# Value, query and key weights loaded ahead of input blocks, five filler products fewer, and new instruction orders

## The chip, the cores and the metric

The kernel runs on one core of a Trainium2 chip. The metric is the device time of one execution in microseconds (us). The core has TensorE (PE in the profile, with PEld for its weight loads), VectorE (DVE), ScalarE (ACT), GpSimd (POOL) and SyncE (SP), which here issues the DMA transfers. Each engine takes its instructions in the order in which they stand, and waits at an instruction until the semaphores it names have come.

## What is computed

Two different layers, each run twice, on 2048 tokens of 448 numbers in bf16. Layer A is attention with 16 heads of 28, in which a token sees eight tokens, two apart, up to itself; layer B is a gated product of width 1792:

```python
def _A_ref(x, wqkv, wo):
    ...
    qkv = (lambda x, *d: x.transpose(*d))((x @ wqkv).reshape(B, S, 3, H, Dh), 2, 0, 3, 1, 4)
    ...
    attn = _softmax(logits, axis=-1)
    o = jnp.einsum("bhsw,bhswd->bhsd", attn, vg)
    return (lambda x, *d: x.transpose(*d))(o, 0, 2, 1, 3).reshape(B, S, D) @ wo

def _B_ref(x, w_gate, w_up, w_down):
    ...
    h = g * u
    return jnp.einsum("bsf,fd->bsd", h, w_down)

x = A_x
x = x + _A_ref(_layernorm(x, axis=-1), A_wqkv, A_wo)
x = x + _B_ref(_layernorm(x, axis=-1), B_w_gate, B_w_up, B_w_down)
x = x + _A_ref(_layernorm(x, axis=-1), A_wqkv, A_wo)
x = x + _B_ref(_layernorm(x, axis=-1), B_w_gate, B_w_up, B_w_down)
return x
```

## The kernel before

The tokens are cut into 16 blocks of 128, held in `x_sb`, and the blocks into chunks (lines 57 and 58): the first layer A has chunks of 256, 512, 512, 512 and 256 tokens, so that chunk 0 is blocks 0 and 1 and chunk 1 is blocks 2 to 5. The line `SEQ` names in which order the chunks of the four layers are gone through. For a chunk of layer A the program does the following.

- Layer norm (`ln_chunk`, from line 582): DVE takes the statistics of each block (L592, L594), ACT makes the scale of two blocks from them by a logarithm and an exponential (L595, L597), DVE writes the normalised block twice into `xn_sb` (L616). In the first layer, PE transposes the block (L631 for the first chunk, with the whole array, L635 for the others, with half of it), and ACT or DVE copies it to `xnTa` (L642, L645).
- Queries and keys (`qk_chunk`, from line 698): four units of 14 products, each in two parts of 6 and 8 products (L355), 256 or 512 columns wide like the chunk, out of `xnTa` and `WQK`. Two products run side by side on the two halves of the array. ACT or DVE takes the result from PSUM to `qk` (L730).
- Values (`v_group`, from line 752): 14 products out of `xnTa` and `WV` in the same two parts, for one or two query blocks of 120 tokens, taken out by L795, L804, L809 and L822.
- Attention (`attn_front`, `attn_back`, `norm`): bursts of 32 or 64 small products (L855, L889) with exponentials on ACT (L864), masks on DVE (L871), and a normalisation by L918 to L939. Then the output projection out of `wo_g` or `wo_h` (`y_blocks`).

A chunk of layer B (`b_chunk`, from line 990) has gate and up products out of `WGU`, their product on ACT and DVE (L1013, L1019), and the down projection out of `WD`.

The weights for queries and keys come to a staging place in `hT` in four loads, one for each group of input rows ("piece" below: c is 1, 3, 0, 2 for the operations 3, 4, 5, 6; L468, shown as L450 by the profile since all plain loads are issued by that helper). Eight copies spread them into `WQK` with gaps for 32-wide heads (L517, two for each piece), on ACT or on DVE, as the order says. Every query and key product of the chunk waits for all eight. Four more copies (L525) rewrite parts of `WQK` once chunks 0 and 1 have read them.

Before there is anything to multiply, PE runs products on zeros, `WARM` of them as a start and `FILL` more as fillers (L509).

No scheduler decides at run time. `ORDER` (line 105) lists for each engine the numbers of the operations in the order in which they are emitted, and `BANKS` (line 162) names the PSUM banks of each of PE's operations; both are tables written out in the file. `schedule` reads them; a bank's next user waits for the operation that gives it back. In PE's table, `a*2.4.5/b:2+c:1` splits the burst `a` after so many groups of eight products and puts there the first steps of `b` and `c` as eight narrow strips each (L358). In SP's table the operations 0, 1, 2 and 7 load blocks 0, 1, 2 to 3 and 4 to 7 of the input, 13 and 12 load blocks 12 to 15 and 8 to 11, 8 and 9 load the value weights, and 3 to 6 the query and key weights. Operations are numbered as they are added, so with five fillers fewer every number behind them falls by five.

Of the kernel before, what the change touches and what calls it, by code (L numbers as in the profile page):

```python
# [59 lines left out]
FILL = 9  # L60
# [37 lines left out]
def grp_nc(g):  # L98
# [21 lines left out]
    ),  # L120
    "act": (
# [262 lines left out]
def build(nc, A_x, A_wqkv, A_wo, B_w_gate, B_w_up, B_w_down, out):  # L384
# [122 lines left out]
    fill = None  # L507
    for n in range(WARM + FILL):
        sc.add("pe", one(lambda E, n=n: E.matmul(ps[:, n % NBK if n < NBK else wb[0], :], warm[:, 0:128], warm, start=True, stop=True), ("warm", n)), 427.0 if n < WARM else 216.0, deps=["c_warm"], mode="F",  # L509
               acquire=wb if n == 0 else None, release=[(wb, 0)] if n == WARM + FILL - 1 else [], prio=-100 if n < WARM else 100, after=fill)  # L510
        fill = sc.ops[-1]
# [650 lines left out]
```

## Time and profile before

| | us |
|---|---|
| median of 3 runs | 379.52 (379.10 to 379.61) |
| the profiled execution | 380.59 |
| its span, from the first to the last instruction | 378.9 |
| PE busy in it | 373.2 |
| DVE busy | 271.6 |
| ACT busy | 199.3 |

The profile is of a single execution. Its times are microseconds from the start of its span; a row of a timeline gives start, duration, engine, line, operation, tiles and how many instructions of that kind follow each other, and in brackets how long the engine was idle before them and what released it. A row of the chain of waits gives start, duration and what stood there. Durations of neighbours overlap: an engine begins the next instruction before the last one's end, so prices are taken from start to start where rows allow it.

### The profile page before, as it was taken

What the parts mean: (1) busy time and instruction counts of PE and PEld (TensorE: products, weight loads), DVE (VectorE), ACT (ScalarE), POOL (GpSimd) and SP (SyncE); (2) the same over time, 40 slices, a digit from 0 to 9 for tenths busy, and PEclk for the clock granted to TensorE, in tenths of its full rate; (3) what the DMA queues carried; (4) which work ended last, traced back from release to release, by engine and by line L of the source; (5) the groups of instructions that cost most, each with busy time, mean ns of one, the idle gap of its engine ahead of it and who ended that gap; (6) DMA issues with size and microseconds to landing.
All of it is one profiled execution on the core that took longest, in us unless ns stands there. A gap on an engine that the chain in (4) does not pass through costs nothing.

```text
span 378.9 us, 14223 instructions
## 1 busy us (share of the span) xinstructions
PE 373.2 (99%) x6372; PEld 208.2 (55%) x6372; DVE 271.6 (72%) x564; ACT 199.3 (53%) x333; POOL 5.2 (1%) x25
## 2 busy tenths in 40 slices
PE   8999999999999999999999999999999999999997
PEld 3554678544544445455766756554455454444864
DVE  6999989988786385867477978528897587275233
ACT  4898786657444565444466413556766544123310
POOL 5000000000000000000000000000000000000000
DMA  7767464610414023022102125220026104103002
GB/s 248 179 139 150 55 185 132 111 23 21 82 22 69 5 55 72 20 48 55 24 10 52 39 43 100 49 51 21 20 32 95 39 3 90 44 2 74 2 13 98
DMA packets 59892, 24.38 MB, mean 64 GB/s; under 512 B 49016, under 2 KB 59704, under 8 KB 59832
## 3 DMA queue, kind: packets, MB, share of 16 engines
q1 hardware_dynamic: 59688, 23.42, 29.0%
q8 instruction: 50, 0.82, 0.9%
q14 instruction: 10, 0.08, 0.1%
q10 hardware_dynamic: 144, 0.06, 0.1%
HBM read 9.04 MB, written 3.50 MB: 33 GB/s over the span
## 4 chain that ended last, share of the span: by engine, by line
PE 92%; ACT 4%; DMA 2%; SPq 1%; DVE 1%; issue 0%; DVEq 0%
PE ps L355 84%; PE ps L358 4%; PE ps L855 2%; ACT qk L730 2%; PE ps L889 2%; DMA hT<-in_A_wqkv_dram 2%; PE ps L1031 1%; SPq L450 1%; ACT E_sb L864 1%; ACT v_sb L822 0%; ACT R_sb L919 0%; ACT R_sb L920 0%; ACT O_sb L900 0%; DVE WQK L517 0%; DVE Qz L841 0%
## 5 line engine op out<-in xcount | busy, mean ns | idle before, releaser
L355 PE MATMUL ps<-xnTb,WGU 64*128 64x512 bf16 (+1 forms) x1902 | 171.6, 332 | 0.8 <-ACT R_sb L920 0.8
L355 PEld LDWEIGHTS ps<-xnTb,WGU 64*128 64x128 bf16 x1902 | 92.2, 94 | 70.3 <-issue 1.5
L1013 ACT ACTIVATE g_sb<-ps 128x512 bf16<-128x512 f32 x112 | 65.8, 596 | 90.7 <-PE ps L355 86.4
L1019 DVE TENSOR_TENSOR hT<-g_sb,ps 128x512 bf16<-128x512 bf16 x112 | 75.1, 681 | 40.1 <-ACT g_sb L1013 38.8
L355 PE MATMUL ps<-WD,hT 64*128 64x448 bf16 x786 | 80.5, 349 | 0.0
L980 DVE TENSOR_TENSOR x_sb<-x_sb,ps 128x448 bf16<-128x448 bf16 x62 | 36.3, 615 | 30.1 <-PE ps L355 29.8
L355 PEld LDWEIGHTS ps<-WD,hT 64*128 64x128 bf16 x786 | 37.7, 94 | 33.7 <-DVE hT L1019 0.2
L355 PE MATMUL ps<-xnTa,WQK 64*128 64x512 bf16 (+1 forms) x496 | 52.6, 353 | 0.5 <-DVE WQK L517 0.2
L864 ACT ACTIVATE E_sb<-ps,shift_sb 128x1024 bf16<-128x1024 f32 (+1 forms) x36 | 37.2, 1068 | 11.7 <-PE ps L855 11.7
L592 DVE BATCH_NORM_STATS2 st<-x_sb 128x6 f32<-128x448 bf16 x64 | 38.2, 618 | 1.4 <-DMA x_sb<-in_A_x_dram 1.2
L355 PEld LDWEIGHTS ps<-xnTa,WQK 64*128 64x128 bf16 x496 | 22.7, 94 | 22.6 <-DVE O_sb L904 1.0
L730 ACT ACTIVATE qk<-ps 128x1024 bf16<-128x1024 f32 (+1 forms) x28 | 25.4, 931 | 17.5 <-PE ps L355 17.1
L616 DVE TENSOR_SCALAR xn_sb<-x_sb,mv,rstd 128x512 bf16<-128x512 bf16 (+1 forms) x64 | 27.6, 455 | 4.9 <-ACT rstd L597 4.9
L871 DVE TENSOR_TENSOR E_sb<-E_sb,MK 128x1024 bf16<-128x1024 bf16 (+1 forms) x36 | 23.4, 658 | 9.0 <-ACT E_sb L864 8.9
L355 PE MATMUL ps<-wo_g,oT 64*128 64x448 bf16 x151 | 26.0, 350 | 0.0
L355 PE MATMUL ps<-WV,xnTa 64*128 64x336 bf16 (+3 forms) x244 | 23.6, 304 | 0.4 <-DMA WV<-in_A_wqkv_dram 0.4
L919 ACT ACTIVATE R_sb<-R_sb 128x960 f32<-128x960 f32 (+1 forms) x18 | 17.3, 961 | 11.4 <-DVE R_sb L918 11.4
L918 DVE STREAM_SHUFFLE R_sb<-O_sb 128x960 f32<-128x960 f32 (+1 forms) x18 | 21.2, 1180 | 0.0
L900 ACT ACTIVATE O_sb<-ps 128x448 f32<-128x448 f32 (+2 forms) x27 | 13.9, 548 | 11.5 <-PE ps L889 11.3
L939 DVE TENSOR_TENSOR oT<-O_sb,R_sb 128x960 bf16<-128x960 f32 (+1 forms) x16 | 17.5, 1095 | 3.2 <-ACT R_sb L920 3.2
L595 ACT ACTIVATE lnv<-mv,eps_sb 128x2 f32<-128x2 f32 (+1 forms) x33 | 9.2, 292 | 20.0 <-DVE mv L594 17.7
L920 ACT ACTIVATE R_sb<-R_sb 128x960 f32<-128x960 f32 (+1 forms) x18 | 17.3, 959 | 0.3
(67 smaller groups left out, 243.2 us busy)
## 6 DMA issues: line engine op xcount, KB each, us to landing
out_dram<-x_sb SPq DMA_DIRECT2D x15, 112.0 KB, 1.8
x_sb<-in_A_x_dram SPq DMA_DIRECT2D x3, 448.0 KB, 7.4
hT<-in_A_wqkv_dram SPq DMA_DIRECT2D x4, 224.0 KB, 5.5
WGU<-in_B_w_gate_dram SPq DMA_DIRECT2D x4, 224.0 KB, 4.1
WGU<-in_B_w_up_dram SPq DMA_DIRECT2D x4, 224.0 KB, 3.8
WD<-in_B_w_down_dram SPq DMA_DIRECT2D x2, 448.0 KB, 4.2
mv_rows<-oT SPq DMA_DIRECT2D x12, 64.0 KB, 1.7
oT<-mv_rows SPq DMA_DIRECT2D x48, 8.0 KB
```

Source lines behind the costliest of these rows:

```text
L355: return lambda E: E.matmul(out(), lhs(), rhs(), start=start, stop=stop)
L592: sc.add("dve", one(lambda E, B=B: E.bn_stats(st6[:, B, :], x_sb[:, B, :]), ("bn", li, B)), 525.0, deps=[("x", li - 1, B)] + ([("xn", li - ...
L616: sc.add("dve", one(lambda E, B=B, dst=dst, src=src: E.tensor_scalar(dst, src, mv[:, B, 0:1], rstd[:, B:B + 1], ALU.subtract, ALU.mult), ( ...
L730: return E.activation(dst, src, ACT.Copy) if hasattr(E, "activation") else E.tensor_copy(dst, src)
L864: return E.activation(E_sb[:, slot, 2 * hp:2 * hp + 2, 0:w], ps[:, b0:b0 + 2, 0:w], ACT.Exp, bias=shift_sb[:, 0:1], scale=SCALE)
L871: return E.tensor_tensor(e, e, MK[:, kind, 0:nc].unsqueeze(1).unsqueeze(1).to_broadcast([128, 2, w // nc, nc]), ALU.min)
L918: sc.add("dve", one(lambda E: E.stream_shuffle(R, Of, [DH] * 32), ("Rs", li, qb)), dve_est(w) + 20.0, deps=[("Oa", li, g)] + prev, prio=prio)
L919: sc.add("act", one(lambda E: E.activation(R, R, ACT.Ln), ("Rl", li, qb)), act_est(w, False), deps=[("Rs", li, qb)], prio=prio)
L939: return E.tensor_tensor(dst, O.rearrange("p d h n -> p h d n"), Rv.rearrange("p d h n -> p h d n"), ALU.mult)
L980: sc.add("dve", one(lambda E: E.tensor_tensor(x_sb[:, B, :], x_sb[:, B, :], ps[:, bk[w], 0:D], ALU.add), ("x", li, B)), dve_est(D), deps=[ ...
L1013: sc.add("act", one(lambda E, gs=gs, bk=bk: E.activation(g_sb[:, gs, :], ps[:, bk[0], :], ACT.Copy), ("G", li, j, f0)), act_est(512), deps ...
L1019: return E.tensor_tensor(hT[:, f0:f0 + nf, hs, 0:nt], v(g_sb[:, gs, :]), v(ps[:, bk[1], :]), ALU.mult)
```

## The change

Outside of `FILL`, `ORDER` and `BANKS` no line differs. PE has 13 products on zeros instead of 18. The orders of PE, ACT, DVE and SP and the banks are written anew; the order of POOL is as it was.

```diff
 WARM = 9
-FILL = 9
+FILL = 4
 YP = 8
...
     "sp": (
-        "0 1 2 7 8 9 5 4 6 3 13 72 12 74 73 10 11 75 76 77 78 196 79 80 198 81 86 84 87 85 71 83 334 336 293 92 82 538 467 333 335 469 89 468 345 91 88 344 466 "
...
+        "0 1 8 9 2 5 4 6 3 7 13 67 12 69 68 10 11 70 71 72 73 74 75 191 76 193 81 79 82 80 66 78 77 331 288 84 328 329 330 340 87 86 533 535 461 463 83 464 339 "
```

Line numbers behind the tables are one higher in the changed kernel (L355 becomes L356). First SyncE's first instructions, the loads: `x_sb` are input blocks, `WV` value weights, `hT` the staged query and key weights. Before:

```order
L450 DMA x_sb<-in_A_x_dram 128x448 x2
L450 DMA x_sb<-in_A_x_dram 128x2x448
L450 DMA x_sb<-in_A_x_dram 128x4x448
L450 DMA WV<-in_A_wqkv_dram 128x2x448 x2
L450 DMA hT<-in_A_wqkv_dram 128x896 x4
L450 DMA x_sb<-in_A_x_dram 128x4x448
L450 DMA WGU<-in_B_w_gate_dram 64x2x896
```

Now:

```order
L451 DMA x_sb<-in_A_x_dram 128x448 x2
L451 DMA WV<-in_A_wqkv_dram 128x2x448 x2
L451 DMA x_sb<-in_A_x_dram 128x2x448
L451 DMA hT<-in_A_wqkv_dram 128x896 x4
L451 DMA x_sb<-in_A_x_dram 128x4x448 x2
L451 DMA WGU<-in_B_w_gate_dram 64x2x896
```

The value weights went ahead of blocks 2 and 3 and of blocks 4 to 7, and the four weight pieces ahead of blocks 4 to 7, which are now the tenth load instead of the fourth (of the two 128x4x448 in the row, the second is blocks 12 to 15, where it was). The next loads stand where they stood.

Then PE from its start to the first wide query and key products. L509 are the products on zeros, L631 and L635 transposes of input blocks, rows with `WV` value products, rows with `WQK` query and key products. Before:

```order
L509 MATMUL ps<-hT 128x512 x14
L631 MATMUL ps<-hT,xn_sb 128x128 x8
L509 MATMUL ps<-hT 128x512 x4
L355 MATMUL ps<-WV,xnTa 128x224 x6
L635 MATMUL ps<-hT,xn_sb 128x64 x8
L355 MATMUL ps<-WV,xnTa 128x224 x8
L635 MATMUL ps<-hT,xn_sb 128x64 x16
L355 MATMUL ps<-WV,xnTa 128x448 x6
L635 MATMUL ps<-hT,xn_sb 128x64 x8
L355 MATMUL ps<-WV,xnTa 128x448 x8
L355 MATMUL ps<-xnTa,WQK 128x256 x6
L355 MATMUL ps<-xnTa,WQK 128x512 x6
```

Now:

```order
L510 MATMUL ps<-hT 128x512 x11
L632 MATMUL ps<-hT,xn_sb 128x128 x4
L510 MATMUL ps<-hT 128x512
L632 MATMUL ps<-hT,xn_sb 128x128 x4
L510 MATMUL ps<-hT 128x512
L356 MATMUL ps<-WV,xnTa 128x224 x14
L636 MATMUL ps<-hT,xn_sb 128x64 x16
L356 MATMUL ps<-WV,xnTa 128x448 x14
L356 MATMUL ps<-xnTa,WQK 128x256 x20
L636 MATMUL ps<-hT,xn_sb 128x64 x16
L356 MATMUL ps<-xnTa,WQK 128x256 x14
L356 MATMUL ps<-xnTa,WQK 128x512 x42
```

Before, the transposes of blocks 2 to 5 (32 products of L635) stood between the value products, ahead of all query and key products. Now those of blocks 2 and 3 (16) stand there, and those of blocks 4 and 5 (the second row of 16) behind the first 20 query and key products.

Last ACT, behind the scales of the first two blocks: L642 and L645 copy transposed blocks, L517 copies query and key weights, L795, L804, L809 and L822 take values out of PSUM. Before:

```order
L595 ACTIVATE lnv<-mv,eps_sb 128x2
L597 ACTIVATE rstd<-lnv 128x2
L645 ACTIVATE xnTa<-ps 128x4x128
L795 ACTIVATE v_sb<-ps 128x4x28
L645 ACTIVATE xnTa<-ps 128x4x128 x3
L795 ACTIVATE v_sb<-ps 128x8x28
L595 ACTIVATE lnv<-mv,eps_sb 128x2
```

Now:

```order
L643 ACTIVATE xnTa<-ps 128x4x128 x2
L596 ACTIVATE lnv<-mv,eps_sb 128x2
L598 ACTIVATE rstd<-lnv 128x2
L518 ACTIVATE WQK<-hT 128x16x28 x3
L796 ACTIVATE v_sb<-ps 128x4x28
L518 ACTIVATE WQK<-hT 128x16x28
L805 ACTIVATE v_sb<-ps 128x8x28
L810 ACTIVATE v_sb<-ps 128x4x28
L518 ACTIVATE WQK<-hT 128x16x28
L596 ACTIVATE lnv<-mv,eps_sb 128x2
L796 ACTIVATE v_sb<-ps 128x8x28
L598 ACTIVATE rstd<-lnv 128x2
```

Five of the eight weight copies came from DVE to ACT, and the copies of transposed blocks 2, 3 and 5 went to DVE. The logarithm in the tenth row and the exponential in the last make the scale of blocks 4 and 5; an eviction of values stands between them. On DVE the order is now: blocks 0 and 1, statistics of 2 and 3, three weight copies, normalisation and transposed copies of 2 and 3, then statistics of 4, 5 and 6, and the normalisation of 4 and 5. In the rest of the program PE has the same products, but in another order; the bursts now hold 75 groups of eight strips instead of 70, and evictions are dealt differently between ACT and DVE.

113 rows, old and new, of tables (BANKS, ORDER) are left out of this document.

## The prediction

> **What bounds the kernel now.** I read the page's first two parts, then busy times by stretch, then the chain of waits and the timelines of the first 15 us, where the change sits.
>
> ```profile
> span 378.9 us, 14223 instructions
> ...
> PE 373.2 (99%) x6372; PEld 208.2 (55%) x6372; DVE 271.6 (72%) x564; ACT 199.3 (53%) x333; POOL 5.2 (1%) x25
> ...
> DVE  6999989988786385867477978528897587275233
> ```
>
> TensorE (PE) is busy for 99% of the span. VectorE (DVE) is at 72% on average, but its row of digits starts 6, 9, 9, 9, 9: until about 47 us it is nearly full too. The table of stretches gives both for one stretch after another:
>
> ```profile
> core 0: us, PE busy (x) PEld busy (x) DVE busy (x) ACT busy (x) POOL busy (x), PEclk, DMA share, GB/s
> 8.00:12.00 4.00, 3.34 (x65) 1.94 (x66) 3.17 (x13) 3.29 (x9) 0.00 (x0) 1.00 1.08 320
> ...
> 12.00:20.00 8.00, 8.00 (x118) 4.75 (x116) 7.78 (x29) 6.36 (x14) 0.00 (x0) 1.00 0.55 122
> 20.00:30.00 10.00, 9.69 (x198) 4.77 (x194) 9.15 (x29) 9.51 (x19) 0.00 (x0) 1.00 0.69 148
> 30.00:40.00 10.00, 9.93 (x188) 5.29 (x186) 8.92 (x15) 7.55 (x10) 0.00 (x0) 1.00 0.68 153
> 40.00:50.00 10.00, 9.16 (x276) 6.04 (x272) 9.73 (x22) 9.31 (x15) 0.00 (x0) 1.00 0.52 89
> 50.00:60.00 10.00, 9.95 (x190) 8.49 (x192) 8.80 (x17) 8.29 (x11) 0.00 (x0) 1.00 0.68 183
> 60.00:370.00 310.00, 309.93 (x5280) 169.91 (x5276) 215.84 (x422) 151.78 (x251) 0.00 (x0) 1.00 0.23 44
> ```
>
> From 12 to 370 us PE idles 0.00 + 0.31 + 0.07 + 0.84 + 0.05 + 0.07 = 1.34 us. A new order can gain no more than that there (and what hides in pipelined matmuls); otherwise only the head can move the end. In the head the chain of waits runs through one queue:
>
> ```profile
> 0.80 0.39 SPq L450
> ...
> 1.71 0.43 SPq L450
> 2.19 0.47 SPq L450
> ...
> 5.23 5.90 DMA hT<-in_A_wqkv_dram
> 11.16 0.66 DVE WQK L517 x3
> ```
>
> SyncE issues the input loads one behind the other; the last piece of the query and key weights, issued at 5.23, lands at 11.13, DVE copies it, and PE begins the query and key products. Its timeline:
>
> ```profile
> 1.25 5.58 PE L509 MATMUL ps<-hT 128*128 128x512 bf16 x14 [1.25 <-DVE hT L480]
> ...
> 7.12 1.03 PE L509 MATMUL ps<-hT 128*128 128x512 bf16 x4
> 8.56 0.46 PE L355 MATMUL ps<-WV,xnTa 64*128 64x224 bf16 x6 [0.42 <-DMA WV<-in_A_wqkv_dram]
> ...
> 10.61 0.29 PE L635 MATMUL ps<-hT,xn_sb 64*128 64x64 bf16 x8
> 10.72 0.94 PE L355 MATMUL ps<-WV,xnTa 64*128 64x448 bf16 x8
> 11.86 1.37 PE L355 MATMUL ps<-xnTa,WQK 64*128 64x256 bf16 x16 [0.20 <-DVE WQK L517]
> ```
>
> PE waits at 8.56 for the value weights and at 11.86 for the copied query and key weights. Fillers only stand in those waits.
>
> **The loads, before and after.** The two loads that move back are in the first two rows, with size and time from issue to landing; below them stand all three 448 KB loads and the two of a single block:
>
> ```profile
> x_sb<-in_A_x_dram SPq DMA_DIRECT2D x1, 448.0 KB, 4.2
> x_sb<-in_A_x_dram SPq DMA_DIRECT2D x1, 224.0 KB, 3.0
> ...
> x_sb<-in_A_x_dram SPq DMA_DIRECT2D x3, 448.0 KB, 7.4
> x_sb<-in_A_x_dram SPq DMA_DIRECT2D x2, 112.0 KB, 2.1
> ```
>
> Blocks 2 and 3 (224 KB, issued 1.71) land at 4.7, blocks 4 to 7 (448 KB, issued 2.19) at 6.4: 448 KB more took 1.7 us. The queue is backlogged (times to landing grow from 3.0 to 5.9), so I substitute equal sums. After the change, blocks 0 and 1, two value pieces and blocks 2 and 3 are 896 KB, what had landed at 6.4: blocks 2 and 3 land at 6.4, 1.7 later, and the value weights, ahead of them, near 5.5 instead of 8.5. Blocks 4 to 7 become the tenth of the same ten loads, so they land when the tenth did, **11.13 instead of 6.4**; the last weight piece, 448 KB ahead, at 11.13 - 1.7 = 9.4. Bounds for blocks 4 to 7: not before that piece, 9.4; not after 13.1, where the next load landed before (5.71 + 7.4, the middle value of three such loads). I take 11.1, the same bytes.
>
> **When PE can start the query and key products.** DVE now makes three weight copies, ACT five, in order behind each other with three value evictions among them. ACT has no such copy now, so its price comes from neighbours:
>
> ```profile
> 9.71 0.26 ACT L795 ACTIVATE v_sb<-ps 128x112 bf16<-128x112 f32 x1
> 9.87 1.66 ACT L645 ACTIVATE xnTa<-ps 128x512 bf16<-128x512 bf16 x3
> ...
> 14.10 0.35 ACT L804 ACTIVATE v_sb<-ps 128x224 bf16<-128x224 f32 x1
> 14.34 0.27 ACT L809 ACTIVATE v_sb<-ps 128x112 bf16<-128x112 f32 x1
> 14.48 1.03 ACT L730 ACTIVATE qk<-ps 128x1024 bf16<-128x1024 f32 x1
> ```
>
> 512 elements go at 0.53 apart, 224 at 0.24, so 448 at about 0.47; bounds 0.22 (DVE's own copies, three in 0.66) and 0.53. The evictions take 0.16 + 0.24 + 0.14. ACT's first copies need the third weight piece, near 8.7: 8.7 + 5 x 0.47 + 0.54 = 11.6 (10.5 to 11.9) instead of 11.86. PE has both value groups behind it by about 11.1, so the products start near 11.6. Five fillers fewer are worth nothing: they stood in front of a wait.
>
> **The new wait.** After 20 of these products PE meets the transposes of blocks 4 and 5, which before ran ahead of them. Two products make a pair of 0.11 (28 pairs in 3.23, next fence), so PE is there at 11.6 + 1.1 = 12.7. Before, the same work was done at 11.86 + 1.1 = 12.96. The transposes need blocks 4 to 7, statistics, a scale and the normalisation:
>
> ```profile
> 9.33 0.73 DVE L616 TENSOR_SCALAR xn_sb<-x_sb,mv,rstd 128x512 bf16<-128x512 bf16 x2
> ...
> 11.72 1.14 DVE L592 BATCH_NORM_STATS2 st<-x_sb 128x6 f32<-128x448 bf16 x2
> 12.78 0.30 DVE L594 BATCH_NORM_AGGREGATE mv<-st 128x2 f32<-128x6 f32 x2
> ```
> ```profile
> 42.26 0.29 ACT L595 ACTIVATE lnv<-mv,eps_sb 128x2 f32<-128x2 f32 x1
> 42.46 0.34 ACT L795 ACTIVATE v_sb<-ps 128x224 bf16<-128x224 f32 x1
> 42.70 0.20 ACT L597 ACTIVATE rstd<-lnv 128x2 f32<-128x2 f32 x1
> ```
>
> Landed 11.13, statistics from 11.16 for 1.36 (11.72 to 13.08) to 12.52; ACT's same three instructions in a row, logarithm, eviction, exponential, 0.64, to 13.20; the first normalisation 0.40 to 13.6, the second to 13.95; the second transpose at 14.0; the next product 0.11 behind it (10.61 to 10.72) at 14.1. The same work was done at 12.96: **1.15 late**. Queued behind the waiting transpose are all of PE's products; ACT's logarithm, waiting from about 11.6 to 12.56, holds back the evictions behind it. Then 14 products (0.77) reach 14.87, while DVE copies block 5's transpose only at 13.95 + aggregate 0.15 + statistics 0.57 + copy 0.4 = 15.05: **0.2 more**. The head costs 1.35.
>
> **What is given back or added later.**
>
> ```profile
> 50.05 3.23 PE L355 MATMUL ps<-xnTb,WGU 64*128 64x256 bf16 x56 [0.81 <-ACT R_sb L920]
> ...
> 66.05 1.49 PE L355 MATMUL ps<-WD,hT 64*128 64x448 bf16 x14
> ```
> ```profile
> 80.84 0.22 PE ps L358 x8
> ```
>
> The largest idle stretch behind the head is 0.81 at 50.05, ahead of the first gate products. The new order has six 256-column query and key products more between the first output projection and that point, three pairs, 0.33: I take **0.33 back** (0 to 0.81). DVE is 2.42 us short of full from 12 to 50 us (8 - 7.78, 10 - 9.15, 10 - 8.92, 10 - 9.73). At 15.05 it will have done some three statistics, one normalisation and five weight copies fewer than before and three transpose copies more, about 2.2 us of work; five weight copies (1.2) it never has to do. So it is 1.0 to 2.2 behind while PE is 1.35 behind: I add **0.2** (0 to 0.9). The replanned bursts hold 75 groups of eight strips instead of 70, each 0.22 in place of a pair at 1.49 / 7 = 0.21: nothing. Stage by stage the rest has the same work on PE under other orders; I take 0, and as bounds what the rows let go, 1.34 of idle time to lose and no ceiling.
>
> Sum: 1.15 + 0.2 - 0.33 + 0.2 = **+1.2 us**. The span becomes 380.1; the profiled execution took 380.59, 1.07 over the median 379.52, to which I add the sum: **380.7 us**.
>
> **The rivals.** (1) *The loads come early; not slower.* What decides is when blocks 4 to 7 land: PE is at the first transpose at 12.7, which is 2.5 behind the landing, so from 10.15 down the wait is gone. Then the head ends at 12.96 as before and 0.33 comes back: 379.2, with copies at 0.53 instead 379.5. For it: from 8 to 12 us the queue moved 320 GB/s, more than the 279 that 2.29 MB make from 2.9 (first block: 0.80 + 2.1) to 11.13. Against it: equal bytes, equal start. [...] With the head's loss swallowed by the 1.34 of idle time this case has 0.25. (2) *The replanned rest gains*: the head costs little and all 1.34 goes: under 378.7, 0.10. (3) *DVE becomes the bound* to 50 us: PE waits for copies and masks, 0.9 more and some new stalls: 381.4 to 382.2, 0.15. (4) *PE's clock.* The first 14 fillers took 0.40 each, the later four 0.26: PE starts slower. If the thinner head lets it fall back for as long as that first stretch (5 us at half rate), 2.5 us are lost: 383.2, 0.05. [...]
>
> **How the numbers follow.** Forecast, 380.2 to 381.4: 0.45; rivals 0.25, 0.10, 0.15, 0.05. A measurement of this kernel tells some 0.2%, 0.76 us, from no change. Slower by more: the forecast's part beyond 380.28 with (3) and (4), 0.65; within: 0.25; faster: 0.10. The range of 379.1 to 382.2 holds the forecast, (1) and (3), and leaves out (2) and (4) and a little of the edges.
>
> **What would show it.** Right: blocks 4 to 7 land near 11, value weights before 6; the first query and key products start by 11.9; PE idles about 0.9 us just ahead of the second pair of half-array transposes, released by a normalisation. Wrong: those transposes without a wait (landing before 10.2); the first wait longer, on ACT's copies (price too low); PE idle in 20 to 50 us above 2 us (rival 3), or pairs of 256 columns at 0.22 (rival 4).

## The result, and the profile after

| | before | after |
|---|---|---|
| time, median (lowest to highest), us | 379.40 (379.10 to 379.61), 4 runs | 385.00 (383.53 to 385.87), 4 runs |
| ratio after to before, 95% interval | | 1.0144 (1.0107 to 1.0181), slower by 1.1 to 1.8% |
| profiled execution, time and span, us | 380.59, 378.9 | 383.53, 381.4 |

The prediction was +1.2 us, slower, with 382.2 as the upper end. Measured are +5.6. The sign was right, the size was not, and the range missed. The two profiled executions differ by only 2.5 us of span: the one of before is a long one, the one of after the shortest of its four. Of 52 further executions of before, timed beside the experiments below, 51 have a median span of 378.0, and one at a granted clock of 0.559, which took 645.29, is left out.

The first rows of the page after are these. PE has more busy time with five fillers fewer, and it is still 98%:

```profile
span 381.4 us, 14275 instructions
...
PE 374.1 (98%) x6397; PEld 208.8 (55%) x6397; DVE 276.1 (72%) x568; ACT 197.2 (52%) x329; POOL 5.2 (1%) x25
...
DVE  5998899998976685877576689546988587365314
```

The table of stretches has the same stretches as before, with PE's busy time first:

```profile
8.00:12.00 4.00, 2.51 (x38) 1.08 (x37) 3.87 (x14) 3.34 (x10) 0.00 (x0) 1.00 1.05 330
12.00:20.00 8.00, 7.88 (x113) 4.67 (x111) 7.61 (x28) 5.93 (x15) 0.00 (x0) 1.00 0.53 129
20.00:30.00 10.00, 9.33 (x211) 5.17 (x204) 9.72 (x35) 9.66 (x19) 0.00 (x0) 1.00 0.57 140
30.00:40.00 10.00, 9.65 (x202) 4.92 (x200) 8.26 (x13) 8.91 (x12) 0.00 (x0) 1.00 0.65 132
40.00:50.00 10.00, 9.94 (x202) 6.01 (x199) 9.50 (x21) 7.26 (x13) 0.00 (x0) 1.00 0.58 119
50.00:60.00 10.00, 10.00 (x266) 8.31 (x266) 9.63 (x19) 8.83 (x12) 0.00 (x0) 1.00 0.52 157
60.00:370.00 310.00, 309.70 (x5288) 170.55 (x5284) 218.55 (x426) 150.16 (x247) 0.00 (x0) 1.00 0.23 45
```

From 12 to 370 us PE idles 0.12 + 0.67 + 0.35 + 0.06 + 0.30 = 1.50 us, against 1.34 before. Read as idle time in these two profiles, almost nothing has changed there, and yet the work ends later. (Three later profiles of after idle for 2.34 to 3.50 us there, one more of before for 1.22, so the first profile of after shows less of the loss than is usual.) So I measured lag: PE's products sorted by their start, each weighed by its columns and its share of the array, fillers left out, and the moment at which the same amount is done. The table gives that moment minus the one in the first profile of before, at four places (labels are those of the experiments):

| execution (span) | at 13 us | at 42 | at 80 | at 376 |
|---|---|---|---|---|
| before, second profile, e9_before_trace (378.6) | -0.29 | -0.34 | -0.33 | -0.25 |
| old orders to 189 us, e8_old_to_189 | -1.24 | -1.12 | -1.22 | (seam) |
| after (381.4) | 0.76 | 1.89 | 1.38 | 2.56 |
| after, e1_again (382.2) | 1.06 | 2.45 | 2.03 | 3.28 |
| after, e16_after_trace (382.7) | 1.32 | 2.98 | 2.74 | 3.82 |
| after, e15_after_trace (384.1) | 1.27 | 3.34 | 4.01 | 5.24 |

Two readings carry the rest of this document. The loss comes in two parts: a **head** of 1.4 to 4.0 by 80 us, which differs from execution to execution, and a **rest** of 1.1 to 1.25 behind 80 us that is nearly the same in all four. And the first profile of before is itself late in its head: with the same orders e8_old_to_189 is 1.2 ahead of it from 13 us on.

The head in PE's timeline, first profile of after:

```profile
7.39 1.08 PE L356 MATMUL ps<-WV,xnTa 64*128 64x224 bf16 x14 [0.61 <-ACT xnTa L643]
9.66 0.61 PE L636 MATMUL ps<-hT,xn_sb 64*128 64x64 bf16 x16 [1.20 <-DVE xn_sb L617]
10.48 1.74 PE L356 MATMUL ps<-WV,xnTa 64*128 64x448 bf16 x14 [0.20 <-DVE xnTa L646]
12.09 1.26 PE L356 MATMUL ps<-xnTa,WQK 64*128 64x256 bf16 x20
13.27 0.61 PE L636 MATMUL ps<-hT,xn_sb 64*128 64x64 bf16 x16
13.72 0.93 PE L356 MATMUL ps<-xnTa,WQK 64*128 64x256 bf16 x14
```

The query and key products start at 12.09 (12.32, 12.40 and 12.35 in the other three), not at 11.6. The 1.20 ahead of the transposes of blocks 2 and 3 comes from the late landing of these blocks. The loads (size, median time from issue to landing; the row of one 224 KB load is blocks 2 and 3):

```profile
x_sb<-in_A_x_dram SPq DMA_DIRECT2D x3, 448.0 KB, 7.0
...
WV<-in_A_wqkv_dram SPq DMA_DIRECT2D x2, 224.0 KB, 3.0
...
x_sb<-in_A_x_dram SPq DMA_DIRECT2D x1, 224.0 KB, 4.5
```

Issued at 2.69, blocks 2 and 3 landed at 7.19; they took 3.0 before. ScalarE's share of the weight copies:

```profile
8.62 0.30 ACT L596 ACTIVATE lnv<-mv,eps_sb 128x2 f32<-128x2 f32 x1 [1.38 <-DVE mv L595]
8.95 0.20 ACT L598 ACTIVATE rstd<-lnv 128x2 f32<-128x2 f32 x1
9.06 1.49 ACT L518 ACTIVATE WQK<-hT 128x448 bf16<-128x448 bf16 x3
...
11.45 0.58 ACT L518 ACTIVATE WQK<-hT 128x448 bf16<-128x448 bf16 x1
```

The copies run 0.47 apart and end at about 12.0, so the weights are ready just as PE comes to them; in the other three profiles PE waits 0.24 to 0.37 for them.

### The profile page after: what moved, and what is told of

Its sections match the earlier page's. It is cut to its first block, busy times and chain, and to the rows that moved or that the text cites. A ratio compares the mean times of both kernels' runs of the same rounds, so it can differ in the third digit from the quotient of the medians.

```text
span 381.4 us, 14275 instructions
## 1 busy us (share of the span) xinstructions
PE 374.1 (98%) x6397; PEld 208.8 (55%) x6397; DVE 276.1 (72%) x568; ACT 197.2 (52%) x329; POOL 5.2 (1%) x25
## 4 chain that ended last, share of the span: by engine, by line
PE 88%; DMA 4%; DVE 3%; SPq 2%; ACT 1%; issue 1%; ACTq 0%
PE ps L356 79%; PE ps L359 4%; PE ps L890 2%; DMA x_sb<-in_A_x_dram 2%; PE ps L856 2%; SPq L451 2%; PE ps L1032 1%; DMA xnTa<-xn_sb 1%; DVE st L593 1%; DMA v_sb<-vt 1%; ACT E_sb L865 1%; DVE hT L1020 0%; DVE xn_sb L617 0%; ACT O_sb L901 0%; DVE xnTa L646 0%
## 5 line engine op out<-in xcount | busy, mean ns | idle before, releaser
L356 PE MATMUL ps<-xnTb,WGU 64*128 64x512 bf16 (+1 forms) x1904 | 171.5, 332 | 0.1
L356 PEld LDWEIGHTS ps<-xnTb,WGU 64*128 64x128 bf16 x1904 | 92.7, 94 | 70.3 <-DVE x_sb L981 1.5
L356 PE MATMUL ps<-WD,hT 64*128 64x448 bf16 x792 | 80.7, 349 | 0.0
L356 PEld LDWEIGHTS ps<-WD,hT 64*128 64x128 bf16 x792 | 38.1, 94 | 33.7
L356 PE MATMUL ps<-xnTa,WQK 64*128 64x512 bf16 (+1 forms) x494 | 53.2, 352 | 0.4 <-DMA xnTa<-xn_sb 0.3
L356 PEld LDWEIGHTS ps<-xnTa,WQK 64*128 64x128 bf16 x494 | 23.3, 94 | 21.2 <-ACT E_sb L865 0.4
L731 ACT ACTIVATE qk<-ps 128x1024 bf16<-128x1024 f32 (+1 forms) x29 | 27.1, 947 | 13.3 <-PE ps L356 13.0
L356 PE MATMUL ps<-wo_g,oT 64*128 64x448 bf16 x154 | 26.3, 349 | 0.0
L356 PE MATMUL ps<-WV,xnTa 64*128 64x336 bf16 (+3 forms) x226 | 22.2, 304 | 1.0 <-ACT xnTa L643 0.6
L920 ACT ACTIVATE R_sb<-R_sb 128x960 f32<-128x960 f32 (+1 forms) x18 | 17.3, 960 | 8.4 <-DVE R_sb L919 8.4
L890 PEld LDWEIGHTS ps<-E_sb,v_sb 64*32 64x32 bf16 x1088 | 13.7, 90 | 8.3 <-issue 3.8
L890 PE MATMUL ps<-E_sb,v_sb 64*32 64x64 bf16 (+1 forms) x1088 | 17.6, 192 | 0.2
```

The lines of the kernel that those rows point to most:

```text
L356: return lambda E: E.matmul(out(), lhs(), rhs(), start=start, stop=stop)
L731: return E.activation(dst, src, ACT.Copy) if hasattr(E, "activation") else E.tensor_copy(dst, src)
L890: ins.append((lambda E, b=b, c=c, o=o, vw=vw, eb=eb, eo=eo: E.matmul(ps[32 * b:32 * b + 32, bk[c], o:o + nc], vw, E_sb[64 * c:64 * c + 64, ...
```

## The experiments

"Orders" are the tables of the change; L numbers and operation numbers are those of the kernel that is named.

**The same kernel once more.** No edit.

> The changed kernel once more, for the spread of its executions (383.5 to 385.9 so far, the profiled one the shortest) and for a second trace. Clock theory: the thinner head lets PE fall back to half rate for a stretch in some executions; then a long execution shows products of 512 columns 0.43 apart instead of 0.21 for some us in the head, and lags about 4.5 us behind the kernel before by 20 us. Rest theory: the head lags 0.8 to 1.2 us in every execution and the spread comes from waits behind 20 us, where transposes by DMA land late; then the lag at 20 us is about 1.1 as in the first trace.

384.83 (384.28 to 384.98), ratio 1.0126 (1.0100 to 1.0152). The loss stands: +5.3 beside 379.57 for before, timed beside it. Its profile gives the second row of after in the table. From 6.4 us on none of its products of 512 columns start 0.43 apart, so the clock theory does not hold. Its lag is 1.06 at 13 us, but 1.90 at 19 and 2.83 at 30, so the 1.1 at 20 us of the rest theory does not hold either.

**Loads or orders?** Two kernels cross them, with the row of SyncE's order alone exchanged:

```
e2_old_loads (in after)      - "0 1 8 9 2 5 4 6 3 7 13 67
                             + "0 1 2 7 8 9 5 4 6 3 13 67
e3_new_loads (in before)     - "0 1 2 7 8 9 5 4 6 3 13 72
                             + "0 1 8 9 2 5 4 6 3 7 13 72
```

> The changed kernel with the ten loads in the order of before (blocks 4 to 7 fourth, value and weight pieces behind them); all else as changed. Loads theory (the head's loss is the late landing of blocks 4 to 7): that wait goes, but the value weights land at 8.5 and the last weight piece at 11.1, ACT's five copies end near 12.5 and the head is still 0.5 to 1 late: 380.5 to 384. Orders theory (the new orders lose by themselves): no better than the changed kernel, 384 to 387. Clock theory: PE idles as long as before in the head, so the spread and the time stay: 384 to 386.

> The kernel before with only the ten loads in the new order; its other orders and its nine fillers as they were. Loads theory: PE meets the transposes of blocks 4 and 5 ahead of all query and key products, so it waits for them until about 13.6 and then still has value and query and key products: 2 to 3 us slower, 381.4 to 382.5. If the later orders carry the loss, it is about as fast as before or 1 us slower: 379.5 to 380.5. Clock theory: nine fillers are there, but PE waits 3 us in one piece: 382 to 385 with a spread.

e2_old_loads: 384.07 (383.25 to 384.94), ratio 1.0109 (1.0077 to 1.0141). e3_new_loads: 385.65 (383.37 to 385.94), 1.0154 (1.0124 to 1.0184). Giving the old loads back to the new orders wins 0.8 of 5.3, with intervals that overlap. Giving the new loads to the old orders loses 6.1. The profiled execution, with a span of 381.6, shows 3.6 of that over the usual 378.0: there VectorE takes the statistics of blocks 2 and 3 ahead of the first normalisation, and PE waits for that in front of its first transposes and of the next ones:

```profile
8.75 0.85 PE L631 MATMUL ps<-hT,xn_sb 128*128 128x128 bf16 x8 [2.90 <-DVE xn_sb L616]
...
12.50 0.29 PE L635 MATMUL ps<-hT,xn_sb 64*128 64x64 bf16 x8 [1.64 <-DVE xn_sb L616]
```

So the old orders do not fit the new loads, and the loss of the change is mostly in what surrounds the loads. Four of the five executions of e3_new_loads also had a mean granted clock of 0.991 to 0.996 and spans of 383.9 to 384.2, the fifth, which is the profiled one, 1.000 and 381.6; what those four did no profile shows. Two of four of e1_again had 0.996 without a longer span. A lower clock, my fourth rival, thus goes with the longer executions of e3_new_loads, but it is not what makes the loss of after, whose first four executions all show 1.000.

**Five fillers back** in after, three ahead of the first value products and two behind them (FILL 9 for 4, later operations renumbered).

> The changed kernel with the five fillers back: three behind the second first-chunk transpose, two behind the first value group, where PE idled 0.6 and 1.2 us. They cost nothing as long as they end inside those waits. Clock theory: PE stays busy enough, the spread shrinks to that of the kernel before (0.5 us) and the time falls by 2 us or more, to 381 to 383. Rest theory: nothing changes, 383.5 to 386 with the same spread.

383.97 (383.57 to 385.57), ratio 1.0114 (1.0081 to 1.0147): 0.9 of 5.3 at most, with intervals that overlap.

**The program cut in two.** At some places PE has done exactly the same operations in both tables. There I joined one kernel's orders ahead of the cut to the other's behind it, for all engines, with the PSUM banks that belong to each.

```
e5_new_to_55     after's tables to PE operation 282 (about 55 us), before's behind it
e6_old_to_55     before's to there, after's behind it
e7_new_to_189    after's tables to PE operation 865 (about 189 us), before's behind it
e8_old_to_189    before's to there, after's behind it
```

> The new orders up to about 55 us on PE (the same 960 products and strips stand before that point in both kernels), with their loads and their eleven and four fillers, and the old orders behind it. The loss is 5.3 us (384.8 against 379.5). Theory A, the head makes all of it (late blocks 4 to 7 and what follows from them): 384 to 385. Theory B, the part to 55 us costs what the two profiled executions show there, 1.1, and some 0.4 lie outside the span: 380.7 to 381.3, the rest of the loss being behind. Theory C, the replanned rest makes all of it: 379.3 to 380.

> The other half: the old orders, loads and fillers up to about 55 us, the new orders behind it. Theory A: 379.3 to 380. Theory B: the rest costs 1.5 in the two profiled executions, and what the typical executions lose beyond those (some 2 us): 381 to 383.5. Theory C: 384 to 385. If the two halves' losses do not add up to 5.3 within 0.8, the seam itself costs or gains.

> New orders up to about 189 us, the old ones behind. Theory A: 384 to 385. Theory B with the loss behind 55 us spread as in the profiled executions (0.4 from 55 to 189, 1.1 behind): 381 to 382.5. Theory C with an even spread of the loss over the rest: 382.

> Old orders up to about 189 us, the new ones behind. Theory A: 379.3 to 380. Theory B: 1.1 from the stretch 190 to 290 us, and up to 1.5 of what typical executions lose more: 380.6 to 382. Theory C, even spread: 382.5.

| kernel | time, us | ratio (95%) |
|---|---|---|
| e5_new_to_55 | 384.88 (383.73 to 386.83) | 1.0122 (1.0095 to 1.0150) |
| e6_old_to_55 | 382.70 (381.91 to 385.99) | 1.0064 (1.0041 to 1.0087) |
| e7_new_to_189 | 400.06 (399.02 to 400.82) | 1.0512 (1.0487 to 1.0537) |
| e8_old_to_189 | 394.84 (394.25 to 396.44) | 1.0386 (1.0360 to 1.0412) |

The times of the last two are those of a bad seam, which I had not foreseen: SyncE's order, cut by what PE needs, brings a transfer of the attention output late. PE's longest wait, first of e7_new_to_189 and then of e8_old_to_189:

```profile
PE ps L303 <- DMA oT<-mv_rows: 13.5, 1, 13.5
```
```profile
PE ps L303 <- DMA oT<-mv_rows: 11.0, 1, 11.0
```

At 55 us the seam costs some 1.5 us on each side: between 55 and 60 us the lag of e5_new_to_55 grows by 1.62 and that of e6_old_to_55 by 1.53, with idle times of 1.45 and 1.37 in front of the first gate products. The two losses, 4.8 and 2.6, are 2.1 more than 5.3, and with the seams taken off 1.0 less. The totals thus decide little, but the lag curves on both sides of a seam do. In e7_new_to_189 the lag is 2.15 at 80 us, and behind the seam, under the old orders, it stays at 18.21 from 217 us to the end (18.20). In e8_old_to_189 it is -1.22 at 80 us, and behind the seam, under the new orders, it grows from 13.28 to 14.44, by 1.16. So the rest goes with the new orders, shown in both directions. That the size is the same as in after is partly chance: 0.83 of the 1.16 lies between 230 and 243 us, where the four profiles of after lose 0.24 to 0.48, and PE has a stop there (0.23 us of idle time, no releaser named) that they lack. The new head, set against an old head of the same batch, costs 2.15 + 1.22 = 3.4. Of the three theories B is nearest, since the loss lies on both sides of the cuts, but the time that it gave e5_new_to_55, 380.7 to 381.3, is too low by 3.6, of which the seam is some 1.6.

**A second profile of before.** No edit, one execution.

> The kernel before, unchanged, for a second profile. Theory P: the profiled execution on which the prediction rests had a head that was some 1.2 us longer than usual (the last weight piece at 11.13, where three later executions with the same order of loads had it at 9.89 to 10.33): span 377.5 to 378.2, last weight piece landed at 9.8 to 10.4, query and key products from 10.6 to 11.1, and from 60 us on the same distance of about 1.2 from the first profile. Rival: the first profile's head is the usual one and the 1.1 over the median lie elsewhere: last piece near 11.1, products from 11.8.

380.34, span 378.6, 0.33 ahead of the first profile and not 1.2. Half right. The last weight piece landed at 10.00, not at 11.13, as in e8_old_to_189 (9.89). But the products began at 11.58:

```profile
1.25 6.16 PE L509 MATMUL ps<-hT 128*128 128x512 bf16 x14 [1.25 <-DVE hT L480]
7.20 0.66 PE L631 MATMUL ps<-hT,xn_sb 128*128 128x128 bf16 x8
...
11.58 5.61 PE L355 MATMUL ps<-xnTa,WQK 64*128 64x256 bf16 x66
```

The same rows of e8_old_to_189 (old orders, transposes at L579):

```profile
5.96 0.85 PE L579 MATMUL ps<-hT,xn_sb 128*128 128x128 bf16 x8
...
10.61 5.73 PE L303 MATMUL ps<-xnTa,WQK 64*128 64x256 bf16 x68
```

In e9_before_trace the fourteen fillers held up the first transposes, whose blocks were normalised by 5.9 and 6.3: the fillers start 0.43 apart until 7.2, while in e8_old_to_189 the distance falls to 0.21 at 4.5, and in the first profile at 6.0. So both profiles of before have a late head, for two different reasons, a late load in one and a late full rate of PE in the other.

**The head, undone in parts.** All three keep PE's new order except as said.

```
e10_head_undone, e11_copies_on_act   SP  "0 1 2 7 8 9 5 4 6 3 ...
e12_late47_repaired                  SP  "0 1 2 8 9 5 4 6 3 7 ...
e10  DVE - 115 113 54 60 55 124 127 126 129 120 118 121 119 136 39 130 133
         + 115 113 120 118 124 127 121 119 54 55 60 61 58 59 57 56 130 133 136 39
     ACT - 116 117 58 59 57 208 61 209 56 122 238 123 239
         + 116 117 208 209 126 122 129 123 238 239
e11  DVE + 115 113 120 118 124 127 121 119 54 60 55 126 129 130 133 136 39
e12  DVE + 115 113 124 127 54 55 60 61 58 59 57 56 120 118 121 119 136 39 130 133
     ACT + 116 117 208 209 126 129 238 239 205 122 123 203 132 202
     PE  - 200 196 201 131 134 197 194 224 230
         + 200 196 201 197 194 195 131 134 224 230
```

(54 to 61 are the weight copies, 124 and 127, 130 and 133 the normalisations of blocks 2 to 5, 131 and 134 the transposes of blocks 4 and 5.)

> The changed kernel with the old order of loads, the five weight copies back on VectorE, and VectorE's and ScalarE's head arranged for that; TensorE's order and the fillers stay new. Theory H (the head's loss of some 3 us is made by late blocks and by the copies on ScalarE together, each hiding the other; the rest costs 1.2 and 0.35 lie outside the span): query and key products from about 11, 381.3 to 382.3. Rival R (TensorE's new order and the missing fillers make the head's loss): 383.5 to 385.

> The same loads, and VectorE's head arranged alike, but the five weight copies on ScalarE as in the changed kernel. Theory H: ScalarE begins with the third weight piece near 9.35 and ends five copies and three evictions later near 12.2, so the products start at 12.3 to 12.5 and the time is 1.0 to 1.5 over the one with the copies on VectorE: 382.5 to 384. Rival: the copies on ScalarE cost nothing (something else starts late as well): within 0.5 of it.

> The changed kernel with blocks 2 and 3 ahead of the value weights again, blocks 4 to 7 still last, all weight copies on VectorE, and the transposes of blocks 4 and 5 behind 42 products instead of 20. It asks whether late blocks 4 to 7 alone can be borne. Theory H: blocks 2 and 3 land at 4.4 instead of 7.2, the products start near 10.6 and not at 12.1, the transposes of blocks 4 and 5 still wait some 0.5: 1 to 1.5 faster than the changed kernel, 383 to 384. Rival: the late blocks bound everything behind them, so nothing is won: 384.5 to 385.5.

| kernel | time, us | ratio (95%) | lag at 80 us |
|---|---|---|---|
| e10_head_undone | 383.12 (382.70 to 384.83) | 1.0094 (1.0070 to 1.0119) | 0.80 |
| e11_copies_on_act | 384.04 (383.50 to 385.34) | 1.0115 (1.0093 to 1.0136) | 1.85 |
| e12_late47_repaired | 384.31 (383.73 to 385.93) | 1.0125 (1.0102 to 1.0148) | 2.27 |

First e10_head_undone, with all copies on VectorE, then e11_copies_on_act:

```profile
8.39 0.57 PE L636 MATMUL ps<-hT,xn_sb 64*128 64x64 bf16 x16
9.98 1.74 PE L356 MATMUL ps<-WV,xnTa 64*128 64x448 bf16 x14 [1.02 <-ACT xnTa L646]
11.55 1.25 PE L356 MATMUL ps<-xnTa,WQK 64*128 64x256 bf16 x20
12.64 0.70 PE L636 MATMUL ps<-hT,xn_sb 64*128 64x64 bf16 x16
13.16 0.94 PE L356 MATMUL ps<-xnTa,WQK 64*128 64x256 bf16 x14
```
```profile
9.77 1.74 PE L356 MATMUL ps<-WV,xnTa 64*128 64x448 bf16 x14 [0.73 <-DVE xnTa L646]
12.59 1.27 PE L356 MATMUL ps<-xnTa,WQK 64*128 64x256 bf16 x20 [1.08 <-ACT WQK L518]
```

The orders of ScalarE differ in one thing more: in e10_head_undone it has the copies of the transposed blocks 2 and 3, which are on VectorE in e11_copies_on_act as in after. The five weight copies on ScalarE, in exchange for these two, cost 1.04 at the start of these products, 1.05 in the lag, and 0.9 in the median time, where the two intervals overlap. From e11_copies_on_act to the kernel after, the loads and VectorE's order for them add about 0.8, across two batches of runs and with intervals that overlap.

e10_head_undone still loses 3.5 and lies between its two theories. Its lag at 80 us, 0.80, is 1.35 less than that of the new head in e7_new_to_189 (2.15) and still 2.0 more than that of the old head in e8_old_to_189 (-1.22). As far as single profiles tell, the larger part of the head's loss thus goes with what was not undone: TensorE's order and the fillers (rival R), and orders of VectorE and ScalarE that are still not before's. Of the 2.0, 1.5 stand at 13 us. The new order puts nothing between the transposes of blocks 2 and 3 and the products that read them, and PE waits 1.02 for the copies (second row of the first list above), so that the query and key products start 0.94 later than in e8_old_to_189. The transposes of blocks 4 and 5, which the old order put among the value products, then take 0.52 more (from 12.64). Giving the five fillers back to after had won 0.9 at most.

e12_late47_repaired won 0.5, not 1 to 1.5: blocks 4 to 7, at 11.5, came so late that moving their transposes back only moved the wait; PE now waits 0.64 at 15.6 us for the copies of those blocks. Both theories that I set down for e12 are thus half right.

**Fewer fillers in before**, because of the head of e9_before_trace: eleven ahead of the first transposes instead of fourteen, and two or four behind.

```
- 41 ... 51 52 53 54 112 115 55 56 57 58 211
+ 41 ... 51 107 110 52 53 206                 (e13_before_11_2, renumbered)
+ 41 ... 51 109 112 52 53 54 55 208           (e14_before_11_4, renumbered)
```

> The kernel before with eleven fillers ahead of the first transposes instead of fourteen, and two behind them instead of four; nothing else. In all traces so far the fillers start at 0.43 apart and go to 0.21 at a moment between 4.2 and 7.2 us that differs from execution to execution; where it is late, fourteen fillers last until 7.2 and hold back the first transposes, which were ready near 6.0. Theory F: that is what makes some executions of before up to 1.2 longer, so eleven fillers (done by 5.95 at the slow rate) take the late ones away: median 378.8 to 379.4, and no execution above 380.5. Rival: the fillers are needed, or the late rate itself costs the time: 379.5 to 380.5.

> Eleven ahead of the first transposes and four behind them. Theory F: as with two, 378.8 to 379.5; where the rate rises late, four fillers at 0.43 end near 8.1 and cost up to 0.4 of what is won. Rival: 379.5 to 380.5.

380.05 (379.16 to 382.14), ratio 1.0006 (0.9981 to 1.0031), and 379.38 (378.91 to 382.44), ratio 0.9985 (0.9962 to 1.0008). Neither can be told from before (379.81 beside them), and both still have executions above 381. The median of e14_before_11_4 lies in the range of theory F, but with executions up to 382.44 the theory that the fillers make the long executions is not borne out, and no version here beats before for certain.

**Two more profiles of after.** No edit, one execution each.

> The changed kernel, unchanged, for a further profile; its executions so far have spans from 381.4 to 383.7 and only the two shorter ones, 381.4 and 382.2, were profiled. Theory: the spread is made ahead of 60 us (late landing of blocks 2 to 7, late rate of TensorE, a late piece of its instructions); from 60 us on it lies at a constant distance from the first profile. Rival: it is spread over the whole span.

> The same once more: under the theory any difference of its span from 381.4 stands at 60 us already, within 0.3; under the rival it grows on behind.

386.18 and 384.77, spans 384.1 and 382.7. Against the first profile of after, e16_after_trace is 1.06 later at 65 us, 1.36 at 80 and 1.26 at the end, as the theory has it. e15_after_trace is 1.45 later at 65 us, 2.63 at 80 and 2.68 at the end, as the theory does not have it: what it adds behind 65 us comes in one wait, for a transpose by DMA, which no other profile of after has (e6_old_to_55 has 0.71 at this place):

```profile
79.96 2.33 PE L356 MATMUL ps<-xnTb,WGU 64*128 64x512 bf16 x20 [0.93 <-DMA xnTb<-xn_sb]
```

They also showed what the long head holds. PE stops in the middle of a group of equal products, and the profile names no releaser. First the first profile of after, then e16_after_trace:

```profile
27.78 0.25 PE L636 MATMUL ps<-hT,xn_sb 64*128 64x64 bf16 x5
28.46 0.22 PE L636 MATMUL ps<-hT,xn_sb 64*128 64x64 bf16 x3 [0.43 <-issue]
```
```profile
33.21 0.31 PE L890 MATMUL ps<-E_sb,v_sb 64*32 64x64 bf16 x18
34.14 0.22 PE L890 MATMUL ps<-E_sb,v_sb 64*32 64x64 bf16 x6 [0.62 <-issue]
```

Counted in PE's instructions in the trace, the first stands ahead of number 705, the second ahead of 961, and 961 - 705 = 256. The page has a DMA queue of its own for instructions:

```profile
q8 instruction: 50, 0.82, 0.9%
```

If the fifty packets of 16 KB hold PE's 12,794 products and weight loads, that makes 256 instructions a packet; this is an estimate from the two counts, and it agrees with the distance between the stops. Gaps of 0.6 to 0.9 between two starts stand at 705 or 961 in all four profiles of after and in four of the seven others with the new head; with the old head in one of seven, e6_old_to_55 (1.94 at 705, where the profile names an exponential of ScalarE that had ended 0.76 before). The packet that would start with number 961 is started behind PE's start of 705, by 0.39 us in the first profile of before (26.83 after 26.44) and by 1.54 in that of after (30.00 after 28.46). Before, it landed 1.5 us after PE's start of 705 and PE came to 961 after 5.4. In e16_after_trace it landed after 3.5, and PE, which now meets a burst of short products there, came to 961 after 4.3 and stood still until 5.1. In all these stops PE went on 1.2 to 1.6 after the landing. That the packet is what PE waits for is inferred from these times and places; no run here changes the packets alone.

## Why the prediction was wrong, step by step

- **Landings.** Value weights 5.0 to 5.8 in the four profiles (predicted near 5.5), last weight piece 9.56 to 9.93 (9.4), blocks 4 to 7 at 10.70, in the other profiles 11.0 to 11.3 (11.13): near in number. Blocks 2 and 3 at 6.9 to 7.2 instead of 6.4: wrong by 0.5 to 0.8. Their sixteen parts landed over 1.7 us (5.48 to 7.19), in the old order over 0.3 to 0.75. Equal bytes did not hold for that load, and the hit at the end of the queue is luck: 11.13 is the tenth landing of a late trace, and in the eight other profiles with the old order of loads it is 9.7 to 10.3. Against those, the same ten loads take some 1 us longer in the new order.
- **Start of the query and key products**, 11.6 predicted, 12.09 to 12.40 measured. The copy was priced rightly (0.47, and 0.47 measured: three in 1.49, one in 0.56). What failed is the start, which I had near 8.7, at the third piece's landing. The piece landed at 8.96 in the first profile and at 9.26 to 9.33 in the others, and the copies began at 9.06 and at 9.28 to 9.36. I also forgot that the scale of blocks 2 and 3 stands ahead of the copies; with those blocks late it ends at 9.15 in the first profile, about as late as the piece. In the others it ends at 8.9 to 9.1 and ScalarE waits for the piece, as in e1_again:

```profile
9.28 1.51 ACT L518 ACTIVATE WQK<-hT 128x448 bf16<-128x448 bf16 x3 [0.38 <-DMA hT<-in_A_wqkv_dram]
```

PE itself was to have both value groups behind it by about 11.1; with blocks 2 and 3 late it came to the query and key products at 12.09 in the first profile without a wait.

- **The wait at blocks 4 and 5.** The point behind their transposes was predicted at 14.1 and came at 13.72, 14.02, 14.22 and 14.28: right in number, and the first rival (loads early) wrong. But the wait stood elsewhere: PE came to them 0.6 to 1.1 later than the 12.7 that I had, and waited there 0.2 at most instead of 0.9. That the point came out right is thus in part luck.
- **VectorE** was given 0.2 and 0.2. The lag grows by 0.4 to 1.1 from 13 to 19 us and by 0.5 to 1.0 more to 42 us, instructions included: too small.
- **The wait at 50.05** was to give 0.33 back and is gone; the lag falls by 0.7 to 0.8 there. Some 0.4 of it is the first profile's own wait, for e8_old_to_189 and e9_before_trace, with the old orders, gain as much at that place.
- **Late instructions**, 0.4 to 0.7 in each profile of after, were in no step.
- **"Stage by stage the rest has the same work on PE under other orders; I take 0."** This step failed: 1.1 to 1.25 in the four profiles of after, and shown by the cut in both directions to go with the new orders. It comes behind 197 us, in the first profile in steps of 0.2 to 0.4 near 208, 241, 269 and 282 us. Most of it is not idle time (0.30 after against 0.07). Among PE's groups from 60 to 372 us, the 864 products of exponentials with values are as many as before and are spread over more time, though one takes no longer (191 and 192 ns); before, and after:

```profile
L889 PE MATMUL ps<-E_sb,v_sb 64*32 64x64 bf16 (+1 forms) x864 | 13.6, 191 | 0.0
L855 PE MATMUL ps<-Qz,qk 64*32 64x64 bf16 (+1 forms) x736 | 11.6, 195 | 0.0
```
```profile
L890 PE MATMUL ps<-E_sb,v_sb 64*32 64x64 bf16 (+1 forms) x864 | 14.7, 192 | 0.2
L856 PE MATMUL ps<-Qz,qk 64*32 64x80 bf16 (+1 forms) x736 | 11.2, 196 | 0.0
```

Part of that is not loss, since the strips were dealt anew too: in this stretch 360 of them stand among the products of exponentials instead of 320, and 216 instead of 240 among the other short products (second rows), which are spread over less time. The rows show where work was moved, and not why the rest is slower.

- **"The profiled execution took 380.59, 1.07 over the median 379.52, to which I add the sum."** This failed too. The excess sat in the head, which is what the change replaces (e8_old_to_189, with the same orders, is 1.2 ahead from 13 us on). The new head had been worked out from that late trace's landings, and then 1.07 was taken off it as if a usual execution of after would be shorter too. The head's loss is 1.4 to 4.0 (mean 2.5) against the first profile and about 3.4 against a usual head of before; the steps that I had for it sum to 1.2.

Added up on the scale of medians: 1.2 as predicted, 1.0 for the wrong base, 1.2 for the rest, 0.5 for instructions, 0.5 to 0.8 for the start of the products, and 0.3 to 0.4 outside the span (time less span is 1.7 to 1.8 in before and 2.0 to 2.2 in after). That makes 4.7 to 5.1 of 5.3 to 5.6; these are readings from single profiles, and 0.2 to 0.9 have no name. What stays open: why the time outside the span differs (e12_late47_repaired has 1.8, e5_new_to_55 2.0 to 2.1, so it goes with something in the head), why the rest, the burst at 208 us and its like, runs slower under the new orders, and the spread of the heads between executions beyond loads, PE's rate and instructions.

Of the rivals none was this case. The third (VectorE becomes the bound) has something for it, since VectorE fills 9.65 to 9.88 of the 10 us from 20 to 30, against 9.15 before. But the sign that I had named for it, more than 2 us of idle time on PE from 20 to 50 us, is not there: the four profiles of after have 1.08 to 1.65.

## What to carry to other kernels

Before a profiled execution is used as the base of a sum, ask in which stage it differs from the usual one, by more profiles (the second one here was late in its head as well); an excess in the stage that the change replaces must not be subtracted again. A re-dealt order of a full engine is not worth zero because little idle time is left: count lag at equal work, since PE lost 1.1 to 1.25 us here behind 80 us, while its idle time there went only from 0.07 to 0.30 in the first profiles. Where short products are moved closer together, look at the packets of the instruction queue as at any other load: here PE stood idle for 0.4 to 0.7 us at each stop that is put down to them by inference.

## What the hardware showed that I had not expected

- PE starts at half its later rate and changes at a moment that the program does not set. The first fillers, 512 columns each, start 0.43 apart and later 0.21; the two profiles of before, the same program, change near 6.0 and 7.2 us, and in eighteen profiles the change comes between 4.0 and 7.3 us, after 6 to 14 fillers, a scatter of 3.3 us. PEclk reads 1.00 throughout. What sets the moment no run here shows.
- Instructions arrive by DMA in 16 KB pieces (50 packets, 0.82 MB) and, as the times above suggest, were late here: the stops at 705 and 961 hold 0.4 to 0.7 us of idle time each in the profiles with the new head and 1.6 in e6_old_to_55. Busy DMA engines alone do not explain it: from 26 to 34 us their share is 0.50 to 0.60 in the four profiles of after, and 0.68 in the first profile of before, which has no such stop.
